# Sparse attention and MoE feed-forward on one core: the first batch's PV matmuls in joined stretches, with the planner's ranks drawn anew

## The chip, the core and the metric

The kernel runs on one core of one Trainium2 chip. The metric is device time in microseconds, the median of several runs. The kernel as a whole is one program: five engines (PE for matmuls, DVE, ACT, POOL, and SP, which here only issues transfers) each work through a fixed queue of instructions in order, and wait on semaphores where an input isn't there yet.

## What is computed

Block-sparse causal attention over 4 batches x 8 heads x 768 positions x 64 dimensions, then a feed-forward layer over the 3072 tokens. Each query takes part in its own block of 64 keys and the blocks with the best gate scores (query times mean key of the block, top 3).

```python
k_rep = k.reshape(B, H, n_blocks, block, D).mean(axis=3)
gate_scores = np.einsum('bhsd,bhnd->bhsn', q, k_rep)      # then causal, then top 3 blocks + own block -> mask
scores = scale * np.matmul(q, k.transpose(0, 1, 3, 2))    # masked, softmax
out = np.matmul(attn, v)
x = out.transpose(0, 2, 1, 3).reshape(B * S, H * D)
h = x @ w_in                                              # 3072x512 @ 512x2048
g = gelu_tanh(h)
return g @ w_out                                          # 2048x512
```

## The kernel before, in words

**Units of work.** Heads are taken in pairs, four pairs to a batch, so pairs 0 to 3 are the first batch (b = 0), 4 to 7 the second, and so on. A pair's loads (q, k, v) are brought in by SP. `pre` (L549) turns k and q by PE (L566, L569) or DVE (L585), makes the block sums `ksb` (L645 from the second batch on), multiplies them with q (the gate matmuls, L693), picks the best blocks on DVE (L709 to L730) and turns the resulting mask on PE (L762) or by a transfer.

**The first batch** is written in `heads2` (L847). A pair has six units (`units`, L839); a unit is a set of (key chunk, first query, width) pieces for both heads. For each unit there is an ST step (L866: scores plus mask, matmuls that use 64 of the 128 rows, two heads side by side, into one of two `wide` PSUM tiles), an exp on ACT (L885, into one of six `at` buffers), a causal select on POOL for units that hold a diagonal block (L911), and PV steps (L934: 128x65 matmuls on all 128 rows, `at` as the stationary operand). There is one PV step per unit and half of the queries (a = 0 or 1: query chunks 0 to 2 or 3 to 5), and a NONE step that gives the `at` buffer back. When all PV steps of a half are done, DVE divides (L952, L953), PE turns the result (L991) and a copy puts it into `xT`.

**The other batches** use `heads` (L1028: ST L1049, exp L1062, select L1076, PV L1088). Each batch ends in `s1` (x @ w_in, L1124, gelu L1136) and `s2` (L1206 for batch 0, L1254 for the others, outputs added on DVE in L1298).

**Weights.** POOL issues the load of w_in in two halves and later w_out in two halves (L485). Ahead of the first half stands a small copy (L482) that waits for another load. A tiny transfer on SP (`held_in`, L493) waits until the first half of w_in has landed; q and k of pair 4 are issued behind it on SP (L427). The copy ahead of w_out waits for q of pair 4, and `held_out` (L493) does for pair 5 what `held_in` does for pair 4.

**What sets the order.** The kernel describes all of this as a list of steps, each with a cost per engine, its inputs and the buffers it takes and gives. `Plan.solve` (L200) runs a list scheduler over them and writes every engine's queue in the order that it found. Where several steps could start at the same time, the lowest number in `RANK` (L21, one number per step) goes first. The numbers are written out by hand from an earlier search. The last steps of the list are 72 filler matmuls (`warm`, L1396, issued at L1401, 128x256 on an identity); they have the highest number, so the planner places one only where it thinks PE has nothing else. The chip knows nothing of the planner's clock: it runs each queue in the order given, fillers too, and waits where it has to.

Of the kernel before, what the change touches and what calls it, by code (L numbers as in the profile page):

```python
# [21 lines left out]
    143, 420, 146, 147, 145, 418, 121, 260, 475, 56, 260, 228, 112, 261,  # L22
    587, 70, 261, 497, 19, 324, 5, 4, 324, 6, 2, 323, 8, 631, 1, 326, 32,
    54, 326, 31, 24, 324, 16, 758, 3, 329, 20, 42, 329, 13, 337, 326, 40,
    367, 372, 329, 30, 355, 38, 955, 1277, 846, 49, 934, 948, 573, 141, 248,
    583, 1191, 645, 590, 118, 241, 117, 242, 240, 198, 61, 119, 83, 613,
    108, 900, 357, 89, 751, 650, 150, 88, 253, 252, 148, 388, 1017, 1315,
    1018, 986, 109, 50, 36, 362, 473, 27, 204, 130, 22, 28, 712, 129, 23,
    21, 832, 236, 135, 265, 286, 124, 209, 428, 151, 520, 230, 325, 351,
    954, 235, 327, 350, 901, 624, 328, 433, 1099, 552, 310, 939, 305, 97,  # L30
    375, 529, 318, 882, 317, 417, 374, 889, 330, 285, 363, 287, 69, 233,
    595, 174, 137, 595, 90, 176, 339, 384, 339, 95, 111, 256, 898, 581, 441,
    280, 110, 897, 629, 923, 227, 474, 352, 298, 258, 543, 921, 62, 259,
    660, 142, 626, 829, 316, 510, 131, 216, 710, 276, 160, 26, 187, 282,
    321, 366, 189, 526, 208, 277, 533, 257, 185, 949, 431, 429, 494, 430,
    577, 331, 268, 641, 278, 838, 381, 625, 273, 289, 320, 462, 237, 465,
    369, 461, 730, 171, 464, 359, 341, 436, 458, 264, 358, 348, 1512, 269,
    456, 364, 398, 937, 213, 432, 361, 365, 360, 864, 460, 251, 219, 639,
    281, 354, 272, 347, 909, 234, 535, 344, 899, 340, 338, 370, 307, 127,
    218, 760, 387, 373, 243, 217, 791, 98, 379, 378, 945, 353, 186, 839,  # L40
    416, 478, 371, 776, 523, 956, 380, 138, 591, 524, 175, 343, 229, 488,
    170, 349, 801, 445, 840, 482, 12, 199, 65, 491, 595, 309, 564, 37, 79,
    85, 80, 84, 713, 17, 1128, 1069, 1232, 283, 284, 1228, 43, 41, 134, 313,
    1093, 1138, 1143, 1171, 755, 9, 559, 314, 400, 579, 288, 477, 466, 476,
    522, 15, 415, 444, 446, 521, 11, 1071, 504, 413, 1094, 25, 585, 512,
    602, 592, 94, 1070, 621, 841, 1072, 7, 593, 530, 528, 642, 14, 489,
    1114, 1319, 484, 10, 578, 414, 409, 485, 39, 493, 471, 454, 499, 18,
    549, 859, 861, 560, 34, 684, 734, 952, 1073, 35, 636, 596, 1102, 677,
    48, 496, 857, 447, 486, 29, 1235, 1257, 1269, 1286, 165, 1248, 778, 990,
    1198, 1220, 1217, 1218, 1223, 308, 203, 291, 211, 190, 715, 721, 1230,  # L50
    51, 172, 1226, 1266, 503, 565, 534, 681, 767, 676, 576, 822, 678, 652,
    653, 759, 770, 786, 612, 536, 911, 787, 792, 793, 800, 916, 917, 1043,
    1249, 126, 125, 222, 293, 295, 303, 292, 300, 226, 158, 689, 690, 736,
    743, 817, 836, 965, 404, 195, 192, 391, 395, 545, 546, 702, 423, 201,
    757, 421, 424, 425, 377, 691, 693, 718, 762, 735, 563, 495, 479, 505,
    541, 519, 619, 1124, 487, 194, 1237, 729, 246, 247, 245, 244, 249, 498,
    584, 427, 383, 604, 795, 794, 1061, 1213, 412, 746, 630, 932, 1321, 440,
    434, 270, 91, 907, 401, 768, 123, 634, 63, 796, 720, 104, 212, 798, 802,
    651, 675, 1040, 72, 724, 896, 46, 1044, 919, 254, 605, 223, 1039, 106,
    615, 294, 667, 744, 178, 668, 774, 924, 597, 68, 1329, 597, 87, 662,  # L60
    597, 173, 205, 52, 53, 81, 82, 77, 396, 76, 773, 989, 531, 86, 78, 918,
    74, 107, 385, 144, 221, 386, 159, 816, 664, 225, 356, 844, 833, 177,
    977, 392, 163, 692, 183, 782, 834, 301, 181, 154, 940, 835, 179, 740,
    393, 164, 705, 402, 538, 890, 335, 599, 103, 156, 599, 115, 169, 599,
    132, 162, 33, 73, 601, 616, 666, 459, 71, 688, 513, 483, 665, 719, 845,
    149, 255, 197, 188, 399, 502, 196, 714, 302, 567, 166, 726, 722, 304,
    206, 622, 75, 394, 506, 128, 717, 716, 306, 224, 765, 723, 290, 220,
    707, 403, 514, 673, 764, 537, 698, 262, 600, 96, 550, 600, 140, 334,
    600, 116, 167, 64, 555, 994, 974, 161, 263, 553, 544, 202, 184, 500,
    501, 728, 297, 59, 210, 279, 518, 152, 312, 1127, 618, 122, 1274, 1216,  # L70
    623, 136, 319, 1214, 406, 1126, 480, 368, 322, 733, 139, 1260, 457,
    1215, 938, 271, 470, 114, 661, 410, 1019, 155, 935, 481, 953, 927, 933,
    1264, 603, 790, 812, 903, 566, 250, 930, 902, 654, 426, 606, 725, 761,
    699, 1666, 872, 1341, 883, 1541, 1060, 1023, 992, 1062, 1645, 928, 904,
    922, 942, 1373, 950, 1063, 1088, 1007, 1178, 711, 685, 814, 819, 1663,
    1542, 92, 448, 905, 1067, 655, 1090, 1101, 1547, 818, 913, 910, 929,
    1394, 1064, 1032, 1029, 1068, 1139, 1056, 1053, 975, 1097, 1182, 468,
    451, 453, 925, 1049, 1013, 1059, 1066, 885, 1006, 1001, 875, 876, 101,
    1225, 914, 1356, 1425, 1275, 1100, 1112, 1255, 1227, 1137, 467, 442,
    881, 912, 1098, 1492, 1494, 1491, 1469, 1579, 1649, 804, 450, 463, 1144,  # L80
    1675, 1766, 1751, 1459, 1605, 1609, 1607, 920, 1689, 1688, 1278, 1389,
    1452, 1468, 1641, 1710, 961, 1680, 1660, 1683, 1697, 967, 737, 749, 100,
    1696, 1754, 1009, 1011, 784, 1031, 1033, 1016, 1025, 1024, 1020, 1132,
    1095, 1045, 1131, 1140, 1146, 1147, 1046, 1221, 1262, 1276, 1263, 777,
    750, 1239, 1241, 1080, 659, 656, 772, 1243, 1083, 695, 979, 57, 779,
    783, 1118, 1160, 754, 1158, 1219, 1298, 1324, 886, 1014, 1440, 1516,
    669, 511, 382, 469, 443, 1209, 570, 753, 868, 1152, 1245, 1314, 703,
    1409, 1538, 1424, 1421, 1461, 1458, 1672, 113, 267, 105, 180, 982, 1771,
    200, 982, 1772, 232, 982, 1775, 342, 299, 58, 60, 207, 67, 539, 93, 828,
    452, 397, 66, 969, 527, 848, 1351, 870, 133, 588, 1642, 1156, 988, 1212,  # L90
    1700, 1606, 991, 1429, 1699, 1698, 1092, 1057, 1010, 1048, 1608, 727,
    1581, 1455, 1578, 1177, 1244, 1532, 1496, 1175, 960, 1602, 936, 617,
    968, 1183, 1366, 1047, 157, 983, 1769, 231, 983, 1768, 756, 983, 1770,
    311, 405, 120, 274, 275, 438, 532, 408, 657, 1234, 492, 906, 435, 542,
    849, 866, 865, 644, 878, 1580, 1206, 1258, 1681, 1390, 1065, 1291, 1701,
    1682, 1194, 1159, 1740, 1026, 1717, 1190, 1419, 1021, 1661, 908, 803,
    1117, 1456, 1106, 1236, 1121, 999, 620, 998, 1089, 996, 1406, 830, 984,
    1773, 558, 984, 1774, 594, 984, 1776, 1489, 411, 437, 1724, 1723, 449,
    407, 873, 877, 884, 1332, 1204, 871, 389, 850, 966, 1005, 419, 895,
    1008, 1353, 1304, 1261, 1224, 1290, 915, 658, 1012, 1203, 1355, 780,  # L100
    1085, 1129, 855, 888, 1240, 1022, 1229, 1523, 1242, 1145, 856, 887, 788,
    1084, 825, 1030, 1289, 860, 1113, 747, 985, 1778, 556, 985, 1777, 540,
    985, 1767, 748, 1331, 1323, 1515, 1514, 1345, 820, 1346, 1526, 957, 962,
    1352, 1326, 731, 853, 1081, 1082, 672, 1252, 607, 1551, 1335, 1015,
    1201, 1561, 507, 1438, 1120, 1256, 1313, 1483, 1125, 1310, 1322, 1312,
    571, 1296, 1325, 1433, 785, 1437, 1119, 1420, 752, 1055, 1155, 1671,
    1259, 1493, 568, 569, 1270, 1272, 1422, 1684, 697, 831, 808, 869, 1611,
    943, 947, 1037, 1036, 1079, 813, 811, 810, 944, 1728, 1674, 1704, 1695,
    1714, 1104, 993, 1096, 1179, 1736, 1115, 1189, 1135, 1136, 1726, 1300,
    1308, 1306, 1318, 1676, 1170, 1168, 1165, 1172, 1721, 1207, 1635, 980,  # L110
    976, 1038, 1111, 1105, 1103, 562, 1233, 1148, 1163, 1281, 1544, 1134,
    1133, 1161, 1166, 1722, 1173, 1002, 1091, 1162, 1693, 1707, 963, 964,
# [167 lines left out]
def kernel(  # L280
# [105 lines left out]
    add = plan.add  # L386
# [460 lines left out]
    def heads2(p):  # L847
        i = p % NB
        base = 100 * p
        pvs = [[], []]  # L850
        for ui, unit in enumerate(units(p)):
            u = (p, 0, ui)
            pr = base + 10 * ui
# [642 lines left out]
```

## Time and profile before

| | |
|---|---|
| time, median of 3 runs | 259.65 us (258.12 to 259.68) |
| the profiled execution's own time | 259.51 us |
| its span, first to last instruction's work | 257.8 us |
| PE busy | 250.8 us (97%), 2530 matmuls |
| DVE busy | 179.6 us (70%) |
| ACT busy | 165.2 us (64%) |
| POOL busy | 86.3 us (33%) |
| last work of the first batch's attention (L934) starts | 42.9 us |
| HBM traffic | 27.26 MB read, 6.29 MB written |

The profile is of one execution. Its page gives busy time by engine, the span in 40 slices, the chain of work that ended last, and groups of instructions; the trace behind it answers for single stretches of time. Times are from the start of the span. Matmuls overlap each other, so that a "busy" PE isn't a PE at its peak; the distance from one matmul's start to the next one's start is what it costs in a stream.

### The profile page before, as it was taken

The page shows a single profiled execution, that of the slowest core. Times are in us where ns is not written, and L with a number is a line of the kernel's source. Part 1 is how long each engine was busy: PE and PEld are TensorE (multiplying, and loading weights), DVE is VectorE, ACT ScalarE, POOL GpSimd, SP SyncE. Part 2 cuts the span into 40 slices and gives each one's busy share as a digit, 9 for nine tenths or more (in the row PEclk, how much of TensorE's full clock was granted, in tenths as well). Part 3 has the DMA queues.
Part 4 walks back from the last instruction along what each step waited for, and adds up shares of the span by engine and source line. Part 5 has one row for each costly group of instructions (what it writes and reads, how often), then busy time and mean ns, then how long its engine had stood idle before and what let it go on. Part 6 is the DMA issues. An engine that isn't in the chain of part 4 may idle for free.

```text
span 257.8 us, 6491 instructions
## 1 busy us (share of the span) xinstructions
PE 250.8 (97%) x2530; PEld 174.8 (68%) x2530; DVE 179.6 (70%) x523; ACT 165.2 (64%) x207; POOL 86.3 (33%) x169
## 2 busy tenths in 40 slices
PE   6799999998999999999999999999999999999997
PEld 5676776564556556556678876556778796667886
DVE  2887863318478999999999999997844462227552
ACT  2359688564789996565989587565898953664000
POOL 8754834003355676223043835100143310000000
DMA  8997898999969997899599694222011152000222
GB/s 159 218 152 161 152 215 132 186 225 185 206 132 212 161 196 159 154 188 174 86 206 194 113 215 99 66 69 51 1 75 42 41 104 83 3 0 0 84 81 84
DMA packets 134095, 32.63 MB, mean 127 GB/s; under 512 B 127696, under 2 KB 130096, under 8 KB 134064
## 3 DMA queue, kind: packets, MB, share of 16 engines
q1 hardware_dynamic: 129328, 27.62, 54.5%
q0 software_dynamic: 3136, 4.19, 10.0%
q10 hardware_dynamic: 1600, 0.39, 0.8%
q8 instruction: 20, 0.33, 0.5%
q14 instruction: 11, 0.09, 0.1%
HBM read 27.26 MB, written 6.29 MB: 130 GB/s over the span
## 4 chain that ended last, share of the span: by engine, by line
PE 71%; DMA 11%; DVE 7%; SPq 7%; ACT 2%; issue 2%; POOL 0%; DVEq 0%; ACTq 0%
PE bank L1254 21%; PE wide L1124 18%; PE wide L1049 10%; PE bank L1206 7%; SPq L427 6%; PE bank L1088 6%; DMA ksd<-in_k_dram 5%; DMA w_in<-in_moe_w_in_dram 4%; PE bank L1401 3%; PE bank L693 2%; DMA qsd<-in_q_dram 2%; PE wide L866 1%; ACT at L885 1%; PE bank L566 1%; DVE sel L725 1%
## 5 line engine op out<-in xcount | busy, mean ns | idle before, releaser
L1124 PE MATMUL wide<-xT,w_in 128*128 128x384 f16 x512 | 87.2, 326 | 0.1
L1136 ACT ACTIVATE G<-wide 128x768 f16<-128x768 f32 x64 | 51.8, 810 | 41.7 <-PE wide L1124 41.7
L1124 PEld LDWEIGHTS <-w_in 128*128 128x128 f16 x512 | 49.3, 98 | 33.2 <-issue 1.9
L1062 ACT ACTIVATE at<-wide 128x896 f16<-128x896 f32 x72 | 63.3, 917 | 10.5 <-PE wide L1049 8.1
L1076 POOL TENSOR_SCALAR_AFFINE_SELECT at<-at 128x256 f16<-128x256 f16 x72 | 31.1, 433 | 66.4 <-ACT at L1062 65.9
L1049 PE MATMUL wide<-qT,kT 76*128 76x512 f16 (+3 forms) x192 | 38.7, 305 | 0.0
L393 POOL CAST kT<-k 64x768 f16<-64x768 f32 x21 | 18.1, 862 | 37.4 <-DVE k L585 30.4
L1254 PE MATMUL bank<-w_out,G 128*128 128x256 f16 x216 | 30.0, 272 | 0.0
L1254 PEld LDWEIGHTS <-G 128*128 128x128 f16 x288 | 26.9, 98 | 4.1
L1298 DVE TENSOR_TENSOR osb<-bank,osb 128x512 f32<-128x512 f32 (+1 forms) x38 | 22.5, 596 | 8.8 <-PE bank L1254 8.2
L1206 PE MATMUL bank<-w_out,G 128*128 128x512 f16 x96 | 25.8, 379 | 0.0
L1088 PEld LDWEIGHTS <-at 128*128 128x128 f16 x504 | 21.6, 98 | 4.3 <-POOL at L1076 0.4
L885 ACT ACTIVATE at<-wide 128x1024 f16<-128x1024 f32 (+3 forms) x24 | 20.8, 917 | 5.5 <-PE wide L866 5.4
L1049 PEld LDWEIGHTS <-kT 76*128 76x128 f16 x192 | 17.5, 98 | 9.7
L1088 PE MATMUL bank<-v,at 128*128 128x65 f16 x504 | 23.8, 194 | 0.0
L1254 PEld LDWEIGHTS <-XS 128*128 128x128 f16 x216 | 20.3, 98 | 3.1 <-issue 0.3
L1254 PE MATMUL bank<-TS,XS 128*128 128x256 f16 x144 | 20.6, 272 | 0.0
L585 DVE STREAM_TRANSPOSE k<-ksd 128x768 f32<-128x768 f32 x12 | 11.6, 969 | 10.2 <-DMA ksd<-in_k_dram 10.2
L1194 DVE TENSOR_TENSOR XS<-G 128x768 f16<-128x768 f16 x12 | 6.5, 550 | 15.2 <-ACT G L1136 15.0
L1401 PE MATMUL bank<-ident 128*128 128x256 f16 x72 | 12.8, 302 | 2.1 <-DVE ident L323 2.1
L972 DVE TENSOR_TENSOR xn<-bank,zr 128x384 f16<-128x384 f32 x24 | 13.4, 558 | 0.8
L1206 PEld LDWEIGHTS <-G 128*128 128x128 f16 x96 | 8.7, 98 | 7.6 <-issue 1.0
(97 smaller groups left out, 322.8 us busy)
## 6 DMA issues: line engine op xcount, KB each, us to landing
out_dram<-osb SPq DMA_DIRECT2D x23, 256.0 KB, 2.0
vsd<-in_v_dram SPq DMA_DIRECT2D x26, 192.0 KB, 3.2
qsd<-in_q_dram SPq DMA_DIRECT2D x48, 96.0 KB, 2.5
ksd<-in_k_dram SPq DMA_DIRECT2D x48, 96.0 KB, 2.5
w_in<-in_moe_w_in_dram POOLq DMA_DIRECT2D x2, 1024.0 KB, 10.7
w_out<-in_moe_w_out_dram POOLq DMA_DIRECT2D x2, 1024.0 KB, 12.5
G<-in_k_dram SPq DMA_DIRECT2D x4, 192.0 KB, 4.6
G<-in_v_dram SPq DMA_DIRECT2D x4, 192.0 KB
```

The costliest lines, as they stand in the source:

```text
L393: nc.gpsimd.tensor_copy(out=out, in_=in_)
L885: nc.scalar.activation(out=T["at", u][:, :, 0:n], in_=plan.buf[("st",) + u].rearrange("p (h w) -> p h w", h=2)[:, :, 0:n], func=AF.Exp, bi ...
L1049: nc.tensor.matmul(st[:, x:e], kT16[i][h][0:76, s0:s0 + 128], qT16[i][h][0:76, s0 + (x - cb):s0 + (e - cb)], start=True, stop=True)
L1062: nc.scalar.activation(out=T["at", u][:, 0:n], in_=plan.buf[("st",) + u][:, 0:n], func=AF.Exp, bias=0.0, scale=SCALE)
L1076: nc.gpsimd.affine_select(out=dg, in_=dg, compare_op=ALU.is_ge, fill=0.0, base=0, pattern=[[0, 2], [1, 128]], channel_multiplier=-1)
L1088: nc.tensor.matmul(pvv[:, qc, 0:65], at[:, cb + (qc - jc) * 128: cb + (qc - jc + 1) * 128], v16[i][:, jc, h, :], start=(gi == 0 and jc == ...
L1124: nc.tensor.matmul(hps[:, 512 * e:512 * e + HALF], w_in16[:, ci, (2 * j + e) * 128: (2 * j + e + 1) * 128], T["xT", b][:, ci, HALF * h:HAL ...
L1136: nc.scalar.activation(out=G[:, :, h, j, :], in_=plan.buf["hps", b, j, h].rearrange("p (e w) -> p e w", e=2)[:, :, 0:HALF], func=AF.Gelu_a ...
L1206: nc.tensor.matmul(plan.buf["ops", b, ti], G[:, f % 2, 2 * ti // NC, f // 2, ti % (NC // 2) * 128:ti % (NC // 2) * 128 + 128], w_out16[:, ...
L1254: nc.tensor.matmul(dst[:, HD * h:HD * h + HD], FACT[m][0][:, j, t * 128:(t + 1) * 128], FACT[m][1][:, j, :], start=(clear and j == 0), sto ...
L1298: nc.vector.tensor_tensor(out=dst(), in0=src(), in1=other(), op=ALU.add)
L1401: nc.tensor.matmul(plan.buf["warm", n][:, 0:256], ident16, z, start=True, stop=True)
```

## The change

Three things are edited. First, in `heads2` the pieces of a unit are collected in `waiting`, one list for each half of the queries, and PV steps are only made after every odd unit (1, 3, 5): a step then holds all pieces of that half from two units, and depends on both units' selects. Both `at` buffers are given back together, after the odd unit's PV steps. A pair then has 4 PV steps where it had 7 (pair 0: 3 where it had 6), the matmuls inside being the same 168 in all. Second, one of the last three stores is issued by ACT and no longer by SP. Third, since the list of steps is 12 shorter, `RANK` has new numbers throughout, and the planner writes new queues for all engines.

```diff
 RANK = [
-    143, 420, 146, 147, 145, 418, 121, 260, 475, 56, 260, 228, 112, 261,
...
-        pvs = [[], []]
+        pvs, waiting, users = [[], []], [[], []], {}
...
-            done = []
+            col = 0
+            for jc, q0, w in unit:
+                for x in range(w // 128):
+                    qc = q0 // 128 + x
+                    waiting[qc // 3].append((af, u, jc, qc % 3, col + 128 * x))
+                col += w
             for a in range(2):
-                cells, col = [], 0
-                for jc, q0, w in unit:
-                    for x in range(w // 128):
-                        qc = q0 // 128 + x
-                        if qc // 3 == a:
-                            cells.append((jc, qc % 3, col + 128 * x))
-                    col += w
-                if not cells:
+                if not waiting[a] or ui % 2 == 0 and ui < 5:
                     continue
-
-                def pv_e(_, u=u, a=a, cells=cells, one=not pvs[a]):
-                    at = T["at", u]
+                cells, waiting[a] = waiting[a], []
+
+                def pv_e(_, a=a, cells=cells, one=not pvs[a]):
...
                 pvs[a].append(add({PE: 0.06 * len(cells) + 0.1}, pv_e,
-                                  [af, ld["v16", p], c_E["ones", i]]
+                                  [x[0] for x in cells]
+                                  + [ld["v16", p], c_E["ones", i]]
                                   + pvs[a][-1:], pr + 0.1 * a,
                                   takes=("pv", ("pv", p, a))))
-                done.append(pvs[a][-1])
-            add({"NONE": 0.0}, lambda _: None, done, pr, gives=[("at", u)])
+                for x in cells:
+                    users.setdefault(x[1], []).append(pvs[a][-1])
+            if ui % 2:
+                for x in (ui - 1, ui):
+                    add({"NONE": 0.0}, lambda _: None, users[p, 0, x], pr,
+                        gives=[("at", (p, 0, x))])
...
-            store([do], 1, 0, 2, SP)
+            store([do], 1, 0, 2, ACT)
```

The queues that the two programs put on the chip can be counted without running them (line numbers of before):

| in the program's order | before | after |
|---|---|---|
| matmuls in all, by line and shape | 2438 | the same 2438 |
| stretches of PV matmuls of the first batch (L934) | 18 | 14 |
| stretches of ST matmuls of the first batch (L866) | 19 | 21 |
| s1 matmuls (L1124) ahead of the gate matmuls of pair 4 (L693) | 114 | 88 |
| fillers (L1401) ahead of that gate / behind it and ahead of the last L1254 / behind the last L1254 | 44 / 8 / 20 | 44 / 28 / 0 |
| POOL: selects (L911) ahead of the first half of w_in (L485) | 9 | 10 |
| selects between the two halves of w_in | 0 | 2 |
| the exp (L885) whose select stands last ahead of w_in | 11th | 13th |

A matmul in fp32 appears twice in the trace, which is why it shows 2530. On SP, the first loads of pairs 1 to 3 come in another order, all eight small transfers of L542 now stand behind the last v load (before, v of pair 2 stood between the fourth and the fifth of them), and from `held_in` on the order (q of pair 4, k of pair 4, `held_out`) is as before. On DVE, the copies of q for pair 1's second half and of pair 0's second mask part (L395), which ACT made before (L391), now stand between the casts of pair 1's k and pair 1's block choice. On POOL two memsets (L532, L533) stand ahead of the select that makes the identity, and the constants of L503 to L514 stand behind the mask table of L521 and L524.

## The prediction

> **What bounds the kernel now.** The page first: PE is busy 97% of the span, so the question is what PE does and where it waits. Its total says little, since the change leaves all 2438 matmuls as they are.
>
> ```profile
> PE 250.8 (97%) x2530; PEld 174.8 (68%) x2530; DVE 179.6 (70%) x523; ACT 165.2 (64%) x207; POOL 86.3 (33%) x169
> ```
>
> Then the timeline of PE in the first batch, for what a stretch of PV costs there (columns: start, duration, engine, line).
>
> ```profile
> 24.18 0.22 PE L866 MATMUL wide<-XS,XS 64*128 64x128 f16 x2
> 24.24 0.22 PE L866 MATMUL wide<-XS,G 64*128 64x128 f16 x2
> 24.39 0.42 PE L934 MATMUL bank<-v,at 128*128 128x65 f16 x8
> 24.75 0.34 PE L866 MATMUL wide<-XS,XS 64*128 64x384 f16 x2
> ```
>
> An ST pair of 128 columns is followed by the next ST pair after 0.06 us (24.18 to 24.24), but by PV after 0.15 (24.24 to 24.39): 0.09 more. Eight PV matmuls need 0.36 until ST goes on, where eight distances of 32 ns inside a stretch make 0.26: again 0.09 to 0.10 more. So each change between 64-row and 128-row matmuls costs about 0.093 us. A PV matmul behind other 128-row work costs its 32 ns and nothing more.
>
> Third, the waits. PE waited for little: 1.5 us for the first mask (L762 at 11.8), 0.6 for the second pair's (18.3), and
>
> ```profile
> PE bank L693 <- DVE ksb L645: 1.2, 1, 1.2
> POOL after_out L482 <- DMA qsd<-in_q_dram: 1.2, 1, 1.2
> ```
>
> The first of these is the gate of pair 4, the first thing of batch 1 that PE needs. So, fourth, the chain of waits into it.
>
> ```profile
> 26.57 0.41 POOL at L911
> 26.97 0.09 POOL after_in L482
> 27.06 9.22 DMA w_in<-in_moe_w_in_dram
> 36.30 0.57 SPq L493
> ...
> 43.30 13.99 DMA ksd<-in_k_dram
> 57.31 0.99 DVE k L585
> 58.32 0.95 DVE ks L628
> 59.28 0.46 DVE kT L395
> 59.74 0.73 DVE ksb L645
> 60.51 0.48 PE bank L693 x8
> ```
>
> This chain is not PE's work: a select lets POOL issue w_in at 27.06, w_in lets SP issue q and k of pair 4, k lands at 57.3 because w_out (issued 42.34) shares the transfer engines with it, and DVE makes ksb. Whatever stands ahead of L693 in PE's queue covers this chain; whatever stands behind it waits. Before, PE arrived 1.2 us too early, with 114 of the s1 matmuls (L1124) as cover.
>
> **What the Trainium skill says.** "TensorEngine Tiling (Array Packing)", Key Properties: changing the tiling mode drains TensorE; the 0.093 us agree. "TensorE: Matmul & The Clock Gate", Part 1: after an idle window (about 3.4 us) PE's clock falls to half until it has been busy as long again. Before shows a cold start: 14 fillers from 2.07 to 5.03 at 0.21 us each, where the last 20 of the kernel take 0.109; no later wait is long enough to show the fall. "DMA: Bandwidth & Descriptors", Issuing engines are not separate DMA queues: all transfers share 16 engines; the 14.0 us of k beside w_out agree, against a median of 2.5 us for later k loads. "SBUF — State Buffer", SBUF: two separate sides: DVE and POOL lock a shared port against each other; DVE's L716 took 0.84 us at 15.35 with POOL busy and 0.28 at 61.44 without.
>
> **The change part by part.**
>
> *Joined PV.* The matmuls stay. 18 PV stretches become 14, but ST falls into 21 stretches instead of 19 (masks and k transposes now cut into it). Counting in the order every change between 64-row matmuls and others: 38 before, 42 after. So 4 x 0.093 = +0.4 us in the first batch, no gain. The 12 steps that vanish cost the chip nothing, only the planner. What joining delays is covered: an `at` buffer is held for one unit longer, but there are six, and by the order each is free about a microsecond before its next exp; were that not so, an exp would wait for PV by about that much.
>
> *The store on ACT.* ACT is empty there; the last store still waits for the last add at 254.8. 0, at most -0.1.
>
> *Work behind the gate.* The new order puts only 88 L1124 ahead of L693, so 26 stand behind it: 26 x 0.163 = 4.2 us of cover moved behind. 28 fillers stand between the gate and the last L1254, before 8: 20 x 0.109 = 2.2; the 20 that ran behind everything, in the shadow of the last store, are gone. They were placed where the planner saw holes; if PE is late, they are plain work. Taking for every pair of neighbours the median start-to-start distance in the trace, all from the gate to the last L1254 is 192.3 before (193.5 in fact, 1.2 of waits) and 199.1 after: +6.8, the two terms above and 0.4 of other neighbours.
>
> *PE's arrival.* By the same sum PE comes to the gate at 52.5 if nothing waits (with fillers starting at 2.45, since two memsets of 0.62 ahead of the identity replace one of 0.24). Waits on the way: the second mask part of pair 0 needs DVE until 13.2, sum 12.5: 0.8. The gate of pair 1 stands behind five DVE operations of 0.55 to 0.7 on the new DVE queue (two k casts with their small products, the q copy that ACT did before), until 15.1: 1.1 more. Masks of pairs 1 and 2, each after L709 to L730 (2.3 us without POOL, 3.3 beside it): 0 to 0.6 each. In all 1.9 to 3.1, I take 2.6, and 1 more for what follows: arrival near 56.
>
> *The chain to ksb.* w_in now stands behind the select of the 13th exp, not of the 11th. Its ST begins at 25.0 by the sum, 27.6 with 2.6 of waits; then 0.5 ST, 0.2 until ACT starts, 1.0 exp, 0.65 select: issue near 30.0, 2.9 late. (With no wait at all 27.4.) Against that, the second half now comes two selects later, about 2.8 us, and v of pair 2 has landed already, so that the first half has the engines more to itself: 8.2 instead of 9.2. It lands at 38.2, 1.9 late. The second half, then in by about 44, is first needed by the 65th L1124, after 51: hidden. The copy ahead of w_in waits for v of pair 3, which SP issues two transfers (1.1 us) later than before, at about 22.7, and so has landed by 27. From there all keeps its order (q, k, w_out on q's landing, DVE, though kT's copy changes places with the sum): 24.2 us as before. The gate runs at 62.4 rather than 60.5: +1.9. PE waits there some 6 us.
>
> *The clock.* Six microseconds of idle PE should cool it. Bounds 0 (it stays warm) and 1.7 (half of 3.4); the cold start above lost 13 x 0.104 = 1.35, which I take.
>
> *POOL's and SP's early queues.* The constants behind the mask table are there by about 8.2 (the distances of before summed in the new order), DVE asks for the first at 8.6: nothing; were they late, the first mask and so w_in would be, by as much. k of pair 1 now comes ahead of its q and lands a microsecond sooner, which the stretch above uses.
>
> *Later waits.* After the gate PE runs 7 to 10 us behind before everywhere, the loads and DVE only some 2, so no new wait should decide; the 1.2 us of old ones I leave.
>
> Sum on the profiled execution, 259.51: +1.9 (gate later) +6.8 (work behind it) +1.35 (clock) = 269.6. The switches (+0.4) and the fillers in the first batch lie ahead of the gate and are swallowed by its wait. The median of the runs is 0.1 above the profiled one, which I neglect.
>
> **Rivals.** (1) *The chain isn't later, or the clock stays warm*: POOL reaches w_in at 27, gate at 60.5, and the wait is too short to cool: 259.5 + 6.8 = 266.3. For it: the new start of the first batch is earlier by a microsecond or two (first ST at 11.6 against 13.72). Against: PE then waits on DVE, and two exps more stand ahead. (2) *The gate isn't waited for, so it is not slower*: k could land early if it gets ahead of w_out. The place is the 14.0 us transfer; without w_out beside it, it needs about 3. It decides if ksb is there before PE arrives at 56, 4.5 us earlier than before. Then 56 + 199.1 + 3.8 (from the last L1254's start to the span's end, 254.05 to 257.8) + 1.7 around it = 260.6; with half of the waits gone 259 and same as before. Against: POOL issues w_out as soon as q lands, at which time SP has only begun with k, and that order is untouched. (3) *It does what it says*: PV stretches go from 18 to 14, two switches each, 8 x 0.093 = 0.7 us saved, with the fillers standing in for waits that vanish: about 258.5. Against: the count of switches went up.
>
> **How the numbers follow.** Main case 0.74, own range 267 to 272.5 (arrival of w_in 27.4 to 31, clock 0 to 1.7). Rival 1: 0.14. Rival 2: 0.09. Rival 3: 0.03. To leave out no more than 2 in 10 the range takes in rival 1 and a late chain: 264.5 to 273. A measurement of this kernel can tell about 1% from no change (257.0 to 262.2). Rival 2 falls within it, rival 3 mostly: faster 0.02, same 0.10, slower 0.88.
>
> **What would show it.** A wait of PE at the first L693 behind s1 of 5 to 8 us, released by ksb, with 88 L1124 ahead; w_in's first issue near 30 and k of pair 4 landing near 59; L1124 at 0.32 for a few us after the wait; as many matmuls as before, 20 fillers more ahead of the last output, and a last stretch without fillers. Wrong it would be if that wait is under 3 us, or if w_in goes out before 27.

## The result and the profile after

| | before | after |
|---|---|---|
| median | 259.44 us (258.12 to 259.68, 4 runs) | 270.21 us (268.79 to 270.31, 4 runs) |
| ratio after to before | | 1.0413, 95% interval 1.0363 to 1.0463 |
| profiled execution's own time, span | 259.51, 257.8 us | 270.25, 268.5 us |
| gate of pair 4 starts | 60.51 us | 61.69 us |
| from there to the start of the last x @ w_out matmul | 193.53 us | 203.02 us |
| from there to the end of the span | 3.76 us | 3.83 us |

The change makes the kernel 4% slower. The three last rows are the sum of the loss: +1.18, +9.49 and +0.07 are the 10.74 us between the two profiled executions.

After's line numbers are one lower than before's up to L847 and three higher from L945: the gate is L692, s1 L1127, s2 L1209 and L1257, PV L931, the select L910, the fillers L1404. The page has PE busy for a smaller share of a longer span, and a PE clock that isn't full everywhere (40 slices of 6.7 us in tenths of full speed; a 9 stands for 90% or more):

```profile
PE 254.3 (95%) x2530; PEld 175.1 (65%) x2530; DVE 178.6 (67%) x526; ACT 164.9 (61%) x205; POOL 86.5 (32%) x168
PEclk9999999965999999999999999999999999999999
```

As many matmuls as before, but 3.5 us more of busy time: some of them ran longer, in slices 9 and 10. The timeline of PE shows that the stretches of PV cost what they did (columns: start, duration, engine, line):

```profile
20.89 0.19 PE L865 MATMUL wide<-XS,G 64*128 64x64 f16 x2
21.02 0.62 PE L931 MATMUL bank<-v,at 128*128 128x65 f16 x14
21.57 0.28 PE L865 MATMUL wide<-XS,XS 64*128 64x256 f16 x2
```

From 21.02 to 21.57 is 0.55, of which 14 x 0.032 = 0.45 is the matmuls: 0.10 for the change of rows, as before. Nothing there explains 10 us. The list of waits does:

```profile
PE bank L692 <- DVE ksb L644: 7.8, 1, 7.8
```

It stood at 1.2 before. The timeline around it, with the idle time in brackets:

```profile
47.69 6.18 PE L1127 MATMUL wide<-xT,w_in 128*128 128x384 f16 x37
61.69 0.76 PE L692 MATMUL bank<-q,ksb 128*32 128x160 f32 x8 [7.83 <-DVE ksb L644]
62.39 4.50 PE L1127 MATMUL wide<-xT,w_in 128*128 128x384 f16 x14
```

PE runs out of s1 at 53.86 and sits still for 7.83 us. The gate then takes 0.76 instead of 0.48, and 14 s1 matmuls take 4.5 us, 0.32 each instead of 0.163. The chain of waits into the gate is the one of before, 1.2 us later at its end:

```profile
26.46 0.82 POOL XS L392
27.28 0.77 POOL v L392
28.06 0.59 POOL at L910
28.65 0.13 POOL after_in L481
28.78 8.26 DMA w_in<-in_moe_w_in_dram
...
44.77 14.20 DMA ksd<-in_k_dram
...
61.45 0.20 DVE ksb L644
```

w_in goes out at 28.78 (27.06 before). It stood behind the select of the 13th exp. That exp ended at 27.94 and two casts ahead of the select on POOL at 28.05, so the casts held it up by 0.1 us at most.

### The profile page after: what moved, and what is told of

Read it like the earlier page. It is cut to its first block, busy times and chain, and to the rows that moved or that the text cites. A ratio compares the mean times of both kernels' runs of the same rounds, so it can differ in the third digit from the quotient of the medians.

```text
span 268.5 us, 6486 instructions
## 1 busy us (share of the span) xinstructions
PE 254.3 (95%) x2530; PEld 175.1 (65%) x2530; DVE 178.6 (67%) x526; ACT 164.9 (61%) x205; POOL 86.5 (32%) x168
## 4 chain that ended last, share of the span: by engine, by line
PE 79%; DMA 8%; POOL 4%; SPq 3%; DVE 3%; issue 1%; ACT 1%; POOLq 0%; ACTq 0%
PE wide L1127 27%; PE bank L1257 20%; PE wide L1052 10%; PE bank L1209 8%; PE bank L1091 6%; DMA ksd<-in_k_dram 5%; DMA w_in<-in_moe_w_in_dram 3%; SPq L426 3%; PE bank L692 2%; PE wide L865 1%; PE bank L1404 1%; PE bank L565 1%; ACT at L884 1%; PE bank L761 1%; POOL G L523 1%
## 5 line engine op out<-in xcount | busy, mean ns | idle before, releaser
L1127 PE MATMUL wide<-xT,w_in 128*128 128x384 f16 x512 | 88.9, 331 | 0.0
L1127 PEld LDWEIGHTS <-w_in 128*128 128x128 f16 x512 | 49.9, 99 | 33.9 <-issue 3.8
L1079 POOL TENSOR_SCALAR_AFFINE_SELECT at<-at 128x256 f16<-128x256 f16 x72 | 32.6, 455 | 82.8 <-ACT at L1065 82.3
L1257 PEld LDWEIGHTS <-G 128*128 128x128 f16 x288 | 27.1, 98 | 4.6 <-issue 0.3
L1257 PE MATMUL bank<-w_out,G 128*128 128x256 f16 x216 | 30.0, 272 | 0.0
L392 POOL CAST kT<-k 64x768 f16<-64x768 f32 x20 | 17.5, 874 | 33.0 <-DVE k L584 32.4
L1209 PE MATMUL bank<-w_out,G 128*128 128x512 f16 x96 | 26.0, 379 | 0.0
L1257 PEld LDWEIGHTS <-XS 128*128 128x128 f16 x216 | 20.1, 98 | 3.2 <-issue 0.5
L1257 PE MATMUL bank<-TS,XS 128*128 128x256 f16 x144 | 20.9, 272 | 0.0
L1404 PE MATMUL bank<-ident 128*128 128x256 f16 x72 | 13.4, 300 | 2.4 <-DVE ident L322 2.3
L692 PE MATMUL bank<-q,ksb 128*32 128x160 f32 (+1 forms) x128 | 7.8, 316 | 7.8 <-DVE ksb L644 7.8
```

Of the source, the lines that this page charges most:

```text
L392: nc.gpsimd.tensor_copy(out=out, in_=in_)
L1079: nc.gpsimd.affine_select(out=dg, in_=dg, compare_op=ALU.is_ge, fill=0.0, base=0, pattern=[[0, 2], [1, 128]], channel_multiplier=-1)
L1127: nc.tensor.matmul(hps[:, 512 * e:512 * e + HALF], w_in16[:, ci, (2 * j + e) * 128: (2 * j + e + 1) * 128], T["xT", b][:, ci, HALF * h:HAL ...
L1209: nc.tensor.matmul(plan.buf["ops", b, ti], G[:, f % 2, 2 * ti // NC, f // 2, ti % (NC // 2) * 128:ti % (NC // 2) * 128 + 128], w_out16[:, ...
L1257: nc.tensor.matmul(dst[:, HD * h:HD * h + HD], FACT[m][0][:, j, t * 128:(t + 1) * 128], FACT[m][1][:, j, :], start=(clear and j == 0), sto ...
L1404: nc.tensor.matmul(plan.buf["warm", n][:, 0:256], ident16, z, start=True, stop=True)
```

## The experiments

Twelve kernels besides after, each compared with before on its own chip (medians of before there: 259.2 to 259.6). "Gate to last" is the stretch from the gate of pair 4 to the start of the last x @ w_out matmul, as in the table.

**1. Cover taken from before (b_gate_early).**

```diff
...
+    g = order.index(last[HP]["gate"][0])
+    mms = [x for x in order[:g] if x in s1_ops and "PE" in x.engines][44:]
+    tail = mms + [x for x in order[:g] if x in s1_ops and set(x.deps) & set(mms)]
+    tail = [x for x in order[:g] if x in tail]
+    order = [x for x in order[:g + 1] if x not in tail] + tail + order[g + 1:]
```

> Before, with 26 of the matmuls x @ w_in of batch 0 moved from ahead of the gate of pair 4 to right behind it (88 ahead, as in after), and nothing else of the change. Theory: the wait at the gate grows from 1.2 to 1.2 + 26 x 0.163 = 5.4 us with the gate still at 60.5, so 263.7 warm, and up to 2.5 more (266.2) if the clock cools in 5.4 us. Rival (the joined PV or the new order elsewhere costs the time): 259.5 as before.

Measured: 265.21 us (264.5 to 265.71), ratio 1.0227 (1.0196 to 1.0257). The timeline at the gate:

```profile
59.21 0.48 PE L693 MATMUL bank<-q,ksb 128*32 128x160 f32 x8 [4.08 <-DVE ksb L645]
59.62 5.59 PE L1125 MATMUL wide<-xT,w_in 128*128 128x384 f16 x23
```

Here ksb came 1.3 us earlier than in the profile of before, so the wait is 4.1 and not 5.4. Gate to last is 199.14, 5.6 more than before: 26 x 0.163 = 4.2 for the moved matmuls, and the rest because PE worked 3.4 us at half clock, in which 11 of them ran. Half of 3.4 would be 1.7, so the two terms together say 0.3 too much. Without one PV matmul moved, about half of the loss is there.

**2. Cover given back to after (a_gate_late).**

```diff
...
+    g = order.index(last[HP]["gate"][0])
+    head = [x for x in order[g:] if x in s1_ops[:80]]
+    cut = [n for n, x in enumerate(head) if "PE" in x.engines][12]
+    head = head[:cut]
+    order = order[:g] + head + [x for x in order[g:] if x not in head]
```

> After, with 24 of the 40 matmuls x @ w_in of batch 0 that stand behind the gate of pair 4 moved ahead of it (112 ahead, as good as before's 114). Theory (the loss is cover that was moved behind the gate, a wait in its place, and a clock that cools in that wait): PE reaches the gate at 53.8 + 24 x 0.163 = 57.7, the gate stays near 61.7, the wait falls from 7.8 to about 3.9, and the time falls by 3.9 us to 266.3, and to about 264 if a wait of 3.9 us no longer cools the clock. Rival (the loss is in the joined PV stretches of the first batch, or in the new order elsewhere): nothing moves, 270.2.

Measured: 267.47 us, with runs from 263.51 to 271.13, so that no ratio is given; the profiled execution took 267.04.

```profile
61.09 0.76 PE L692 MATMUL bank<-q,ksb 128*32 128x160 f32 x8 [2.79 <-DVE ksb L644]
61.78 1.03 PE L1212 MATMUL bank<-w_out,G 128*128 128x512 f16 x2
64.13 0.71 PE L761 MATMUL bank<-ident,madd 128*128 128x128 f16 x5 [1.31 <-DVE madd L729]
```

The gate's wait falls by 5.0 us to 2.8. Not all of it is won: the moved matmuls had also covered the next wait, that of the mask made from the gate (1.31 us, none in after), and the clock still falls. The theory's direction holds, and its sum lacked that second wait. In the four runs the mean clock over the span is 0.998, 0.987, 0.987 and 0.981, in the order of their times: with a wait of this length it differed from run to run how much of what follows ran slow, and in the fastest run hardly any of it did. The four runs overlap with those of after, so how much is won stays open.

**3. The clock alone (a_keep_warm).**

```diff
...
+        for n in range(66):
+            nc.tensor.matmul(plan.buf["gt", HP, 0][:, 0:256], ident16, z,
+                             start=True, stop=True)
...
```

> After, with 66 dummy matmuls of 128x256 (about 7.2 us) into the gate's own bank right ahead of the gate of pair 4; they add nothing to the result. Theory: they fill the 7.8 us wait and no more, so the clock stays at full rate, the 14 matmuls x @ w_in behind the gate take 0.163 instead of 0.320 each and the gate itself 0.5 instead of 0.76: 2.5 us less, 267.7. If the clock is no reason, or the dummies outlast the wait: 270.2 or more.

Measured: 267.57 us (266.9 to 268.12), ratio 1.0319 (1.0287 to 1.035), 2.6 less than after.

```profile
54.38 7.37 PE L1469 MATMUL bank<-ident 128*128 128x256 f16 x66
61.94 0.48 PE L692 MATMUL bank<-q,ksb 128*32 128x160 f32 x8 [0.20 <-DVE ksb L644]
62.35 2.45 PE L1127 MATMUL wide<-xT,w_in 128*128 128x384 f16 x14
```

The gate is no earlier (61.94), but takes 0.48 again, and the same 14 matmuls 2.45 instead of 4.50. Gate to last is 200.64: the cold clock costs 203.02 - 200.64 = 2.4 us.

**4. The fillers behind the gate (a_no_fillers).**

```diff
...
+    g = order.index(last[HP]["gate"][0])
+    order = order[:g] + [x for x in order[g:] if x not in fillers]
```

> After, without the 28 fillers that stand behind the gate of pair 4 (fillers touch no output). Theory: behind the gate PE never waits, so each is plain work: 28 x 0.109 = 3.05 us less, 267.2. Rival (they stand in holes, as the planner meant): 270.2.

Measured: 270.53 us (267.97 to 272.02), ratio 1.0401 (1.0341 to 1.0461): nothing won. The theory fails here, and the rival is right. PE's waits in this kernel are:

```profile
PE bank L692 <- DVE ksb L644: 7.9, 1, 7.9
...
PE wide L1052 <- DVE qT L394: 0.6, 1, 0.6
PE wide L1127 <- ACT G L1139: 0.6, 1, 0.6
PE bank L1257 <- DVE XS L1197: 0.3, 1, 0.3
PE bank L1257 <- ACT G L1139: 0.3, 1, 0.3
```

The lower four aren't in after's list. They lie at 114.9 and from 135 to 138, where after has 23 of its 28 fillers (112.9 to 114.6, 134.6 to 137.6), at the turns of ACT between exp and gelu. Gate to last stays at 203.06 (203.02 in after). Of the 3.05 us of the 28 fillers, 1.8 come back as these waits and some 0.3 as half clock: from the gate on PE worked 5.5 us at half clock here, 4.9 in after. The other 0.9 or so isn't traced. So the fillers stand for the most part in holes of the new order, and the time is lost to the holes. Why the new order has them and the old hardly any wasn't taken apart.

**5. The chain's head (a_w_in_early).**

```diff
...
+    g = order.index(w_in_ops[0])
+    pool = [x for x in order[:g] if x.eng == "POOL"]
+    order.remove(w_in_ops[0])
+    order.insert(order.index(pool[-3]), w_in_ops[0])
```

> After, with the issue of the first half of w_in moved on POOL ahead of the last three steps that precede it (two casts and the select of the 13th exp), so that it stands behind the select of the 11th exp, as in before. Theory: it is issued near 26.5 instead of 28.8, q, k, w_out and ksb follow 2.2 us earlier, the gate runs near 59.5, and all behind it moves along: about 268.0. If something else than the issue of w_in sets when ksb is there: 270.2.

Measured: 268.16 us (267.72 to 268.6), ratio 1.0335 (1.0288 to 1.0383). In its chain of waits:

```profile
26.65 9.52 DMA w_in<-in_moe_w_in_dram
...
59.77 0.76 PE bank L692 x8
```

w_in goes out 2.1 us earlier, the gate runs 1.9 earlier, and the time falls by 2.0. The issue of w_in does set the gate, as the chain says.

**6. No wait at the gate (a_k_first): the second rival, made on purpose.**

```diff
...
-            [ld["q", HP]], 40, None if x else ("q", HP))
+            [ld["q", HP]], 40, None if x else ("k", HP))
+        w_out_ops.append(issued["out"])
...
+    order = [x for x in order if x not in w_out_ops]
+    g = order.index(issued["k", HP]) + 1
+    order[g:g] = w_out_ops
```

> After, with w_out issued by POOL behind k of pair 4 (the copy ahead of it waits for k instead of q), so that k has the transfer engines to itself: the second rival's mechanism, made on purpose. Theory: k lands near 48, ksb near 51, so PE, which arrives at 53.8, doesn't wait; no cold clock; gate to last x @ w_out matmul 203.0 - 2.5 = 200.5, so 54 + 200.5 + 3.8 + 1.7 = 260.0, up to 2 more if w_out, issued some 4 us later, is late for its first use. If k's 14 us are not due to w_out: 270.2.

Measured: 260.86 us (259.5 to 261.78, 20 runs), ratio 1.006 (1.0044 to 1.0077).

```profile
51.69 3.09 PE L1127 MATMUL wide<-xT,w_in 128*128 128x384 f16 x18
54.71 0.48 PE L692 MATMUL bank<-q,ksb 128*32 128x160 f32 x8
55.12 2.45 PE L1127 MATMUL wide<-xT,w_in 128*128 128x384 f16 x14
57.50 0.59 PE L1209 MATMUL bank<-w_out,G 128*128 128x512 f16 x2
```

The gate follows s1 without a gap: ksb was there at 51.2, since k, with w_out issued at 46.5, was in by 48.6 instead of 59.0. With no other edit, 9.4 of after's 10.8 us are gone. (Before gains from it too, 1.05 us in experiment 8.) All that the change did on PE ahead of the gate, the joined stretches among it, is still in this kernel. w_out's first half landed at 57.46 and was first used at 57.50: not waited for, by a hair.

**7. The same on before (b_k_first), and with the joining alone (b_k_first_join).** The first has the edit of experiment 6. The second also moves each even unit's PV matmuls:

```diff
...
+        order.remove(op)
+        order.insert(m - 1, op)
...
```

> Before with the same: w_out behind k of pair 4. Theory: the gate's wait of 1.2 us vanishes, 258.3. If w_out is then late for its first use, or k isn't held up by w_out: 259.5 or more.

> Before with w_out behind k of pair 4, and the PV matmuls of even units moved to right ahead of those of the odd unit after, without a new search: 12 stretches of PV where before has 18, and 34 changes between 64-row and 128-row matmuls where it has 38. Theory (a change costs 0.093 us, PE bounds the stretch once the gate isn't waited for): 4 x 0.093 = 0.4 us less than w_out behind k alone, within the noise. Rival (joining is worth 0.7 or more by itself): 0.7 to 1.5 us less.

Measured: 264.02 us (263.38 to 264.55), ratio 1.0174 (1.0135 to 1.0213), and 264.61 us (263.5 to 266.28), 1.0199 (1.015 to 1.0248). Both expectations missed by over 5 us. The chain of waits of b_k_first has the cause:

```profile
37.95 0.41 POOL at L911
38.35 4.89 issue
...
43.26 0.19 POOL after_out L482
43.45 1.73 POOL w_out L485 x2
45.17 0.43 POOL at L911
...
45.66 0.36 PE bank L934 x6
```

In before's order one select of the first batch stands behind the place where w_out was put. POOL waited for k with that select behind it, PE's PV waited 3.44 us for the select, and after it PE worked at half clock from 46.86 to 50.27. In after's order no select was left behind that place.

**8. w_out behind k and also behind the last select (b_k_first2), with the joining alone (b_k_first_join2), without fillers (b_k_first_lean2).**

Against experiment 7 the place of w_out differs:

```diff
...
-    g = order.index(issued["k", HP]) + 1
+    g = max(order.index(x) for x in selects + [issued["k", HP]]) + 1
```

> Before with w_out issued behind k of pair 4 and also behind POOL's last select of the first batch, so that the copy that waits for k holds up no select. Theory: the 3.4 us wait of PE for that select and the 1.3 us of cold clock after it, which w_out behind k alone brought, vanish, and so does the gate's old wait of 1.2: about 258.2. Rival (w_out some 2 us later is late for its first use, or k waits for something else): 259.5 or more.

> The same with the PV matmuls of even units moved to right ahead of those of the odd unit after (12 stretches where before has 18, 34 changes of rows where it has 38), no new search. Theory: 4 x 0.093 = 0.4 us less than without the joining if nothing waits, so within the noise, and up to 1 more if an exp or a division that comes later is waited for. Rival (joining is worth something by itself): 0.7 to 1.5 us less.

> The same as w_out behind k and the last select, without the 44 fillers that stand behind the first ST matmul (16 in the first batch, 8 later, 20 behind the last x @ w_out matmul; fillers touch no output). If fillers are plain work: 24 x 0.109 = 2.6 us less. If they stand in real holes, as the 28 in after turned out to: no change within the noise.

| | median | ratio to before |
|---|---|---|
| b_k_first2 | 258.36 us (22 runs) | 0.9962 (0.9943 to 0.9982) |
| b_k_first_join2 | 258.92 us (14 runs) | 0.9994 (0.9973 to 1.0015) |
| b_k_first_lean2 | 257.27 us (8 runs) | 0.9938 (0.9915 to 0.9962) |

The first is what was expected: no wait at the gate, 1.05 us less than before.

```profile
56.79 2.60 PE L1127 MATMUL wide<-xT,w_in 128*128 128x384 f16 x15
59.32 0.48 PE L693 MATMUL bank<-q,ksb 128*32 128x160 f32 x8
```

In the second, 12 stretches instead of 18 change nothing that can be measured; the gate runs at 59.55 and gate to last is 193.53 against 193.23, so the joining alone isn't worth even its 0.4. PE has three short waits there that the first doesn't have (0.09, 0.11 and 0.13 us), as much as the four changes of rows should save. The third lies between its two theories: 24 fillers (2.6 us) ahead of the last matmul are gone, and by the trace 0.40 us ahead of the gate (58.92 for 59.32) and 0.47 behind it (192.76 for 193.23) come back. It is the fastest kernel of this study, though its interval overlaps with that of the first.

**9. The store alone (b_store_act).**

```diff
-            store([do], 1, 0, 2, SP)
+            store([do], 1, 0, 2, ACT)
```

> Before with only one of the last three stores issued by ACT instead of SP, as in the change. Theory: the last store still waits for the last add, the stretch from the last x @ w_out matmul to the end stays 3.8 us, 259.5. Rival: the three stores' issue on one queue was part of the end, 0.3 to 0.6 us less.

Measured: 258.85 us, ratio 0.9991 (0.9964 to 1.0018); from the last matmul's start to the end 3.82 us. Nothing, as predicted.

## Why the prediction was right, and which terms were not

The main case came in: cover moved behind the gate, a wait in its place, a clock that cools in the wait, and no gain from the joining. Of its own sum, 259.51 + 1.9 + 6.8 + 1.35 = 269.6, against 270.25 for the profiled execution:

- **Gate later: +1.9, measured +1.18.** w_in was put near 30.0 and went out at 28.78. The step that was too big is the 2.6 us of waits put into the first batch: the ST of the 13th exp began at 26.26, not at 27.6. That is still 1.26 behind the sum of 25.0, while PE's gaps ahead of s1, other than the wait for the first filler, sum to under half a microsecond (the largest is 0.15); the rest of the 1.26 isn't taken apart. Experiment 5 shows that the issue sets the gate. The rest of the chain was right: 8.26 us for the first half of w_in (8.2), and 24.65 from its landing to the gate (24.2). But +1.18 is one pair of profiles. In the three profiles with before's chain whose gate waits (before and experiments 1 and 9) it runs at 59.21 to 60.51, in the four with after's chain (after and experiments 2, 3 and 4) at 61.09 to 62.22; the means differ by 1.9.
- **PE's arrival: near 56, measured 53.86**, for the same reason: of the 2.6 + 1 put in for waits on the way, 1.4 came. That made the wait 7.8 and not some 6, and cost nothing by itself: PE's early arrival is idle time ahead of a fixed gate.
- **Work behind the gate: +6.8, measured 9.49 - 2.38 (clock) = 7.1.** The 4.2 for the 26 s1 matmuls fits experiment 1, to 0.3. The 2.2 for fillers has the right size and the wrong cause: "if PE is late, they are plain work" fails in experiment 4. A filler in a hole that moves along with everything else stays in its hole.
- **The clock: +1.35, bounds 0 to 1.7, measured +2.4** (experiment 3). This is the term that was sized wrong: the bound took half of one idle window of 3.4 us. The windows below show why it can be twice that.
- **Switches +0.4, swallowed; later waits as before; the store 0:** PE's idle time behind the gate sums to 0.12 us, the joined stretches show no gain in experiment 8, and the store none in 9.

-0.7 for the gate, +1.0 for the clock, +0.3 for the work and +0.1 at the end are the 0.7 us by which the sum fell short. It is in part luck that the sum came so near: the terms for the gate and for the clock are off in opposite directions.

**The rivals.** The first (chain not later, or clock warm, 266.3) is out: both parts happened. The third (it does what it says) is out by experiment 8: joining alone is worth nothing here. The second (k ahead of w_out, no wait) did not happen, but its mechanism is right: 260.6 was worked out for it and 260.86 measured when it was brought about. That the number fits so well is luck: PE came to the gate at 54.71 and not at 56, and the work behind it took 200.73 and not 199.1. So most of the loss is the price of waiting at one gate: of the 10.8 us, 9.4 go with that wait. What the change costs with the wait gone from both kernels is 2.5 us (260.86 against the 258.36 of b_k_first2). The s1 matmuls that moved cancel there. The gate comes 4.6 us earlier and the work behind it takes 7.5 longer, 4.2 of which is these matmuls and 2.2 the 20 fillers that used to run behind the last of it.

## What to carry to other kernels

When work is taken out ahead of a gate that is fed by a chain of transfers, nothing is won unless the chain gets shorter too; ask what the chain's length is and how much work lies ahead of the gate, before counting instructions. A small load that is needed soon belongs ahead of a large one that is needed later, but look at what else stands behind the instruction that is made to wait for it. And a wait of some 3 us on PE can have a second price, in the clock of what follows.

## What the runs showed of the hardware

The granted clock falls and rises on a grid of 3.41 us: in after the first rise came at 5.16, the next changes at 56.36, 66.60 and 267.99, which is 15, 3 and 59 times 3.41 apart. Busy time in windows cut where the clock changes shows it (stretch, length, then busy us and instructions of PE, PEld, DVE, ACT and POOL, then the granted clock, the DMA share and GB/s), first of after:

```profile
52.95:56.36 3.41, 0.91 (x6) 0.33 (x4) 0.00 (x0) 1.27 (x2) 0.00 (x0) 1.00 1.43 216
56.36:59.77 3.41, 0.00 (x0) 0.00 (x0) 0.78 (x1) 0.00 (x0) 0.00 (x0) 0.50 1.28 232
59.77:63.18 3.41, 1.49 (x11) 0.63 (x12) 2.42 (x6) 0.00 (x0) 1.14 (x1) 0.50 0.63 106
63.18:66.60 3.42, 3.42 (x13) 1.59 (x11) 1.40 (x13) 0.00 (x0) 0.00 (x0) 0.50 0.99 173
66.60:70.01 3.41, 3.41 (x26) 2.18 (x25) 0.97 (x2) 2.10 (x3) 0.00 (x0) 1.00 0.29 65
```

Then of b_gate_early:

```profile
56.56:59.97 3.41, 0.76 (x11) 0.37 (x12) 2.71 (x5) 0.00 (x0) 1.05 (x2) 0.99 0.93 178
59.97:63.38 3.41, 3.41 (x12) 1.62 (x11) 2.98 (x15) 0.81 (x1) 0.83 (x2) 0.50 1.05 170
63.38:66.79 3.41, 3.41 (x22) 2.06 (x21) 0.00 (x0) 1.70 (x3) 1.41 (x2) 1.00 1.13 213
```

In after PE was at half clock for three such windows, in b_gate_early for one, in a_gate_late for two. The window at whose end the clock fell wasn't an idle one: PE was busy for 0.91 us of it in after, 0.76 in b_gate_early and 1.37 in a_gate_late. The clock came back only after one whole window in which PE was (nearly) always busy, so a window in which PE resumes halfway counts as lost too: in after PE worked from 61.69 to 66.60, 4.9 us, at half clock, and half of that is the 2.4 us of experiment 3. In b_gate_early the clock fell 0.7 us after PE had gone back to work. The fall came 2.0 us (a_gate_late) to 4.8 us (b_gate_early) after PE went idle. A wait of 2.8 us was long enough in the profiled run of a_gate_late, though not in its fastest run; 1.2 in before was not. "TensorE: Matmul & The Clock Gate", Part 1, of the Trainium skill says that the window is 3413 ns long and free-running; the 3.41 us agree, and so does the spread from 2.0 to 4.8. The bound in the prediction left out "free-running". As an estimate from these traces, PE works through one to two windows at half clock after a long wait (3.4 us in b_gate_early, 4.9 in after), which costs half of that, 1.7 to 3.4 us.

The other is k's 14 us. Beside w_out, k of pair 4 took 14.2 us in after; with w_out issued behind its first part, it was in some 3 us after its last issue at most (45.5 to 48.6). "DMA: Bandwidth & Descriptors", Queues, rings and completion order, of the Trainium skill says that an engine goes round its queues packet by packet. The trace of after agrees. From 49 to 56 us, with w_out on POOL's queue (q0) and k on SP's (q1), they moved (packets, MB, share of 16 engines):

```profile
q0 software_dynamic: 1292, 1.31, 110.9%
q1 hardware_dynamic: 1280, 0.16, 29.7%
```

That is one packet for one packet, but k's have about 128 bytes and w_out's about 1024, so k got 11% of the bytes. That other packet sizes would end the 14 us wasn't tried.
